# A gated long-convolution and MLP kernel: a filter fold in three operations, a product unit split by output block, and a new instruction order

## The chip, the cores and the metric

The kernel runs on one core of a Trainium2 chip. A core has five engines with an instruction queue of its own each: TensorE (PE, matrix products into the banks of PSUM), VectorE (DVE, elementwise work), ScalarE (ACT, activations and copies with a scale), GpSimd (POOL) and SyncE (SP). Here POOL computes reciprocal square roots and issues accumulating transfers, and SP issues most other transfers. Engines run beside each other and wait for one another through semaphores.

The metric is the device time of one execution in microseconds. Before the change the median of three runs is 221.62 us (221.31 to 222.36). A smaller time is better.

## The reference

The input is a block `x = A_q` of 2048 tokens by 640 features in bf16. The output mixes two branches by a gate per token: branch A, a long convolution over tokens by FFT, and branch B, a layer norm, a GELU product, shifts by one or two tokens, a second product, and an MLP.

```python
def _A_ref(q, k, v, shift_k, ssm_k, ssm_D):
    ...                                    # k_shift: 4 taps over tokens, per feature
    kv = k_shift * v
    kv_pad = jnp.pad(kv, ((0, 0), (0, S), (0, 0)))
    kf_pad = jnp.pad(ssm_k, ((0, 0), (0, S)))
    ...                                    # kv_f, kf_f: real FFTs of length 2 S over the tokens
    y_f = kv_f * kf_f[None, :, :, :]
    y = ...                                # inverse FFT, the first S tokens, in bf16
    y = y + kv * ssm_D[None, None, :]
    return q * y

def _B_ref(x, w1, w2, w3, w4):
    h = _gelu(_layernorm(x, axis=-1) @ w1)
    ...                                    # four quarters of h, shifted by +1, -1, +2, -2 tokens
    hs = jnp.concatenate([g0, g1, g2, g3], axis=-1) @ w2
    x1 = x + hs
    h2 = _gelu(_layernorm(x1, axis=-1) @ w3) @ w4
    return x1 + h2

g = _sigmoid((x * gate_w).sum(-1, keepdims=True))
return g * a + (1 - g) * b
```

The term `kv * ssm_D` is a convolution too, whose filter has D at its first place and zeros elsewhere; so D can be added to the first element of the filter `ssm_k`.

## The kernel before

**Branch A.** The 640 features are five chunks of 128, one feature per partition; `c` is a chunk from 0 to 4. Per chunk, `chunk(c)` (line 1102) issues these steps in turn. `h_load` loads the filter of 2048 taps as four blocks of 512. `h_fold` (line 763) folds each block onto itself, sums and differences of mirrored halves, so that a transform of half the size does. A DMA transpose turns the fold; `h_even` and `h_chunk` finish the filter's transform with products by constant tables (`Re_h`, `Ro_h`, made in `_folded_dft`) and ACT copies the results into `HF`. `k_load`, `v_load`, `kv`, `kv2`, `x_fwd` and `combine` do the same for `k_shift * v`, into `XF`. `unit(c)` (line 1017) then multiplies the two transforms of a chunk: there are four blocks of each, a block of the output is the sum over pairs of an input and a filter block, and each complex product is formed from three real ones (arrays `ACC` and `TT`, with three parts). It works through two halves, output blocks 2 and 3 first and then 0 and 1; in a half, `a` runs over the filter blocks. Some of the sums `ACC += TT` are not DVE instructions but accumulating transfers on POOL. At the end of a half, two operations write the real and imaginary part of the two output blocks into `XF` and a third sets one partition's row. `final(g, o, q, k)` (line 1043) does the inverse transform of output block `o` for group `g` of chunks (chunks 0 to 2, then 3 and 4) by PE, with ACT, DVE and a second PE product (`flip`) behind it, multiplies by q and the gate, and adds it to the output.

**Branch B.** `ln1`, `mm1`, `mm2`, `ln2`, `mm3` and `mm4` do the norms and products of B over 16 tiles of 128 tokens. In `mm1` (line 929) four feature blocks of 128 go into `hT`; the 32 features left over of each quarter come together as a fifth product, and four copies of 32 partitions put them into `hT` at the shift of their quarter (line 946 on DVE, line 944 as a transfer on SP). `mm2` adds onto `X` (line 980, DVE). `base(t)` scales a tile's first 384 columns and stores them to the output through SP; `mm4(t)` overwrites that tile of `X` on ACT and accumulates it onto the output through POOL.

**The order.** The functions only record operations. `schedule` (line 271) then issues them in the order of a list, `SEQUENCE` (line 486), which holds the number of every operation; each engine's queue follows that list. `PLACES` (line 546) says which PSUM bank each product gets, and `ON` (line 553) switches single operations between two engines, in the order in which `turn` (line 677) was called: a scaled copy between ACT and DVE, a sum between DVE and a transfer, a copy of `mm1` between DVE and SP. `emit` (line 301) finds which earlier operations each one depends on and puts in the waits.

The helpers `tt` (line 660), `ts` (line 665) and `act` (line 670) record most operations, so one line of the profile holds many; PE's products are line 692.

Of the kernel before, what the change touches and what calls it, by code (L numbers as in the profile page):

```python
# [407 lines left out]
def _folded_dft():  # L408
# [22 lines left out]
            np.where(first, np.sin(np.pi * kodd / 2), -np.sin(w * 2 * kodd * p))]  # L431
    alt, one = (-1.) ** p, p == 0
    even[0][:, 0:1], even[1][:, 0:1] = (alt - 1) / 2, 0
    even[2][:, 0:1], even[3][:, 0:1] = one, (alt + 1) / 2
    odd = [np.cos(w * bo * p), -np.cos(w * bo * n1), -np.sin(w * bo * n0), -np.sin(w * bo * n1)]
    Rh = np.concatenate(even + odd, 1)
# [10 lines left out]
def bass_gated_mix__ssm_conv_h3__mixer_s_mlp__prompt_kernel(  # L447
# [34 lines left out]
    def ps(n, cls):  # L482
# [3 lines left out]
    SEQUENCE = [1, 4, 5, 6, 26, 7, 3, 45, 24, 8, 0, 49, 50, 51, 55, 48, 68, 9, 10, 11, 12, 13, 14, 15, 16, 69, 17,  # L486
# [66 lines left out]
    ON = ("0000000011111111011011111111111100010000010000101111000000000000001000010010000100000100000100000000"  # L553
          "0000000000000000000000000000000")

    HW = S + 4
    oXF = alloc(20480)
# [611 lines left out]
```

## Time and profile before

| | |
|---|---|
| median of three runs | 221.62 us (221.31 to 222.36) |
| profiled execution | 222.27 us |
| its span, first to last instruction | 220.2 us |
| DVE busy, instructions | 212.1 us (96%), 418 |
| PE busy, matmuls | 209.0 us (95%), 1401 seen |
| ACT busy, instructions | 196.5 us (89%), 326 |
| POOL busy, instructions | 45.7 us (21%), 48 |

The profile is one execution. An engine is busy while an instruction of it runs; a wait is put down to what ended it. In a row of the timeline the first number is the start in the span and the second the duration; several instructions of one shape that follow each other are merged, with their count after x. In a row of groups, the two numbers behind the count are the busy time in us and the mean duration in ns, and then the idle time just before them. A few matmul records are missing from the trace.

### The profile page before, as it was taken

What the parts mean: (1) busy time and instruction counts of PE and PEld (TensorE: products, weight loads), DVE (VectorE), ACT (ScalarE), POOL (GpSimd) and SP (SyncE); (2) the same over time, 40 slices, a digit from 0 to 9 for tenths busy, and PEclk for the clock granted to TensorE, in tenths of its full rate; (3) what the DMA queues carried; (4) which work ended last, traced back from release to release, by engine and by line L of the source; (5) the groups of instructions that cost most, each with busy time, mean ns of one, the idle gap of its engine ahead of it and who ended that gap; (6) DMA issues with size and microseconds to landing.
All of it is one profiled execution on the core that took longest, in us unless ns stands there. A gap on an engine that the chain in (4) does not pass through costs nothing.

```text
span 220.2 us, 3837 instructions
## 1 busy us (share of the span) xinstructions
PE 209.0 (95%) x1401; PEld 125.7 (57%) x1410; DVE 212.1 (96%) x418; ACT 196.5 (89%) x326; POOL 45.7 (21%) x48
## 2 busy tenths in 40 slices
PE   6899999999999999999999999999999999999961
PEld 2598755554664446665446565456665445776730
DVE  5999999999999999999999999999999998999993
ACT  2499999999999999999999999999798978558981
POOL 1331102400010001001380103331101060645440
PEclk9999999999999999999999999999999999999995
DMA  6999998999979995898486893793198299366696
GB/s 170 346 233 214 246 207 231 177 236 193 284 246 204 383 198 95 162 174 185 120 147 110 201 193 43 163 174 71 19 160 182 65 219 246 39 74 71 74 179 119
DMA packets 79440, 37.73 MB, mean 171 GB/s; under 512 B 59001, under 2 KB 76990, under 8 KB 79422
## 3 DMA queue, kind: packets, MB, share of 16 engines
q1 hardware_dynamic: 73920, 31.91, 63.3%
q0 software_dynamic: 5328, 5.51, 18.9%
q8 instruction: 11, 0.18, 0.3%
q10 hardware_dynamic: 174, 0.07, 0.2%
q14 instruction: 7, 0.06, 0.1%
HBM read 14.88 MB, written 5.77 MB: 94 GB/s over the span
## 4 chain that ended last, share of the span: by engine, by line
DVE 57%; PE 28%; DMA 5%; ACT 5%; issue 3%; SPq 0%
DVE arena L660 46%; PE PSall L692 28%; ACT arena L670 5%; DVE arena L665 4%; DMA arena<-arena 3%; DVE arena L861 3%; DVE arena L980 2%; DMA arena<-in_A_q_dram 2%; DVE arena L946 1%; DVE arena L862 0%; DVE arena L866 0%; SPq L237 0%; DVE arena L735 0%; DVE arena L704 0%
## 5 line engine op out<-in xcount | busy, mean ns | idle before, releaser
L692 PE MATMUL PSall<-arena 128*128 128x512 bf16 (+5 forms) x1340 | 201.7, 309 | 3.4 <-ACT arena L670 1.3
L660 DVE TENSOR_TENSOR arena<-arena 128x1024 bf16<-128x1024 bf16 (+14 forms) x270 | 175.1, 712 | 1.7 <-DMA arena<-arena 0.9
L692 PEld LDWEIGHTS PSall<-arena 128*128 128x128 bf16 x1349 | 121.6, 98 | 82.7 <-ACT arena L670 3.3
L670 ACT ACTIVATE arena<-PSall 128x512 bf16<-128x512 f32 (+7 forms) x157 | 94.1, 659 | 9.6 <-PE PSall L750 4.9
L670 ACT ACTIVATE arena<-arena 128x640 bf16<-128x640 bf16 (+5 forms) x107 | 93.5, 904 | 1.9 <-DVE arena L660 1.8
L237 POOL DMA_DIRECT2D out_dram<-arena x24 | 24.1, 1133 | 67.7 <-ACT arena L670 51.7
L869 POOL TENSOR_TENSOR arena<-arena 128x2 f32<-128x2 f32 (+2 forms) x15 | 17.3, 1157 | 58.0 <-DVE arena L866 42.3
L670 ACT ACTIVATE arena<-PSall,arena 128x640 bf16<-128x640 f32 (+2 forms) x32 | 20.5, 652 | 6.8 <-PE PSall L692 6.6
L237 POOL DMA_DIRECT2D arena<-arena x5 | 4.9, 978 | 43.2 <-DVE arena L660 43.2
L980 DVE SCALAR_TENSOR_TENSOR arena<-PSall,arena 128x640 bf16<-128x640 f32 x16 | 12.9, 816 | 0.3
L665 DVE TENSOR_SCALAR arena<-arena 128x640 bf16<-128x640 bf16 (+6 forms) x35 | 11.9, 358 | 0.1
L861 DVE BATCH_NORM_STATS2 arena<-arena 128x6 f32<-128x320 bf16 x20 | 9.0, 484 | 1.3 <-DMA arena<-in_A_q_dram 1.3
L715 PE MATMUL PSall<-arena 128*128 128x512 bf16 x15 | 5.4, 529 | 2.2 <-DVE arena L712 2.2
L670 ACT ACTIVATION_READ_ACCUMULATOR arena<-arena 128x1 f32 x28 | 5.7, 204 | 0.0
L946 DVE TENSOR_SCALAR arena<-arena 32x256 bf16<-32x256 bf16 (+1 forms) x22 | 5.3, 240 | 0.4
L715 PEld LDWEIGHTS PSall<-arena 128*128 128x128 bf16 x15 | 1.8, 128 | 5.0 <-issue 2.5
L922 PE MATMUL PSall<-arena 128*128 128x128 bf16 x40 | 3.4, 220 | 0.9 <-DVE arena L665 0.9
L922 PEld LDWEIGHTS PSall<-arena 128*128 128x128 bf16 x40 | 2.4, 97 | 1.3 <-DVE arena L665 1.3
L866 DVE SCALAR_TENSOR_TENSOR arena<-arena 128x2 f32<-128x2 f32 (+2 forms) x19 | 2.9, 155 | 0.0
L718 ACT ACT_TABLE_LOAD x1 | 1.3, 1283 | 1.3 <-PEq L1154 1.3
L862 DVE BATCH_NORM_AGGREGATE arena<-arena 128x2 f32<-128x12 f32 x10 | 1.7, 192 | 0.0
L980 DVE DVE_READ_ACCUMULATOR arena<-PSall,arena 128x1 f32 x16 | 1.3, 80 | 0.0
(19 smaller groups left out, 2.9 us busy)
## 6 DMA issues: line engine op xcount, KB each, us to landing
arena<-in_A_ssm_k_dram SPq DMA_DIRECT2D x5, 512.0 KB, 5.2
arena<-in_A_q_dram SPq DMA_DIRECT2D x6, 320.0 KB, 5.7
arena<-in_B_w_dram SPq DMA_DIRECT2D x1, 1920.0 KB, 8.4
out_dram<-arena SPq DMA_DIRECT2D x16, 96.0 KB, 3.9
arena<-arena POOLq DMA_DIRECT2D x4, 384.0 KB, 5.0
out_dram<-arena POOLq DMA_DIRECT2D x16, 96.0 KB, 3.6
arena<-in_A_q_dram SPq DMA_DIRECT2D x8, 192.0 KB, 4.1
out_dram<-arena POOLq DMA_DIRECT2D x8, 192.0 KB, 4.0
```

Source lines behind the costliest of these rows:

```text
L237: fn = lambda e: e.dma_start(out, in_, **kw)
L660: P.op(eng, lambda e: e.tensor_tensor(o, real(a), real(b), op), [a, b], [o], dve_ns(o, [a, b], 2) if eng == "dve" else 500)
L665: P.op(eng, lambda e: e.tensor_scalar(o, real(a), s1, s2, op0=op0, **({} if op1 is None else {"op1": op1})), [a] + aps, [o], dve_ns(o, [a] ...
L670: P.op("act", lambda e: e.activation(real(o), real(a), f, bias=bias, scale=scale, **({"accum_out": accum} if accum is not None else {})), ...
L692: fns.append(lambda e, l=l, r=r, i=i: e.matmul(real(o), l, r, start=(i == 0), stop=(i == last)))
L715: P.op("pe", lambda e: e.matmul(real(pw), warm[:, 0:128], warm[:, 128:640], start=True, stop=True), [warm], [pw], 427.0 if i < 14 else 216.0)
L861: P.op("dve", lambda e, o=o, i=i: e.bn_stats(o, i), [i], [o], 400)
L866: P.op("dve", lambda e: e.scalar_tensor_tensor(o, a, x, b, op0=op0, op1=op1), [a, b] + aps, [o], n_of(o) / 0.96 + 65)
L869: P.op("pool", lambda g: g.tensor_tensor(o, a, e, ALU.pow), [a, e], [o], dur)
L922: P.op("pe", [lambda e, c=c, pb=pb, xn=xn: e.transpose(real(pb)[:, 128 * c:128 * (c + 1)], xn[:, 128 * c:128 * (c + 1)], ident) for c in r ...
L946: P.op("dve", lambda e, o=hT[q, 4, c0:c0 + n], i=hx[q, :]: e.tensor_scalar(o, i, 1.0, None, op0=ALU.mult), [hx[q, :]], [hT[q, 4, c0:c0 + n ...
L980: P.op("dve", lambda e: e.scalar_tensor_tensor(x, real(pr), 1.0, x, op0=ALU.mult, op1=ALU.add, accum_out=st[1, 0][:, t:t + 1]), [pr, x], [ ...
```

## The change

There are four parts.

1. **The fold.** The D term is no longer added to the filter's first element by an operation of its own. A small constant array `skip` holds zero and D, and the third operation, which used to copy the two unpaired elements of each block, adds `skip` to them. The two large operations now run over 128 elements where they ran over 127, and so also produce the element that two small operations made; its sign in the difference is the other one, and the constant tables turn it back. The last run writes one element beyond the fold, so each chunk of `HF` gets 16 elements of padding (`HS`).
2. **The last half of unit 4.** For chunk 4 output blocks 1 and 0 are worked out one after the other instead of together.
3. **The copies of `mm1`** on DVE now name the neighbouring column of `hT` as read, so that they wait for the block before.
4. **Order, banks and switches.** `SEQUENCE` and `PLACES` are new lists, and `ON` differs in three places: of the tokens 768 to 1023 the last copy moves from SP to DVE, of the tokens 1024 to 1535 the second moves from SP to DVE and the third from DVE to SP.

```diff
+    even[5][0] *= -1
...
+    odd[1][0] *= -1
...
-    HW = S + 4
+    HW, HS = S + 4, 4096 + 16
...
-    oHF = alloc(20480)
+    oHF = alloc(5 * HS)
...
-    dgT = bfs[:, 32:42]
-    Dcol, gwT = dgT[:, 0:5], dgT[:, 5:10]
+    skip = bfs[:, 0:40].rearrange("p (c e b) -> p c e b", c=5, e=2)
+    gwT = bfs[:, 48:53]
...
+    P.op("dve", lambda e: e.memset(skip, 0.0), [], [skip], 70)
...
-    act(dgT, pr, ACTF.Copy)
+    act(skip[:, :, 1, 0], pr[:, 0:5], ACTF.Copy)
+    act(gwT, pr[:, 5:10], ACTF.Copy)
...
     def h_fold(c):
         k, fo = kst[c], kfo[c]
-        tt(k[:, 0, 0:1], k[:, 0, 0:1], Dcol[:, c:c + 1], ALU.add)
         kh = k.rearrange("p b (h i) -> p b h i", h=2)
-        fh = fo.rearrange("p e b (h i) -> p e b h i", h=2)
         for e, op in ((0, ALU.add), (1, ALU.subtract)):
-            tt(fh[:, e, :, :, 1:128], kh[:, :, :, 1:128], kh[:, :, ::-1, 255:128:-1], op)
-            tt(fo[:, e, :, 128], k[:, :, 384], k[:, :, 128], op)
-        ts(fo[:, :, :, 0], kh.rearrange("p b h i -> p h b i")[:, ::-1, :, 0], 1.0, None, ALU.mult)
+            f = fo[:, e, :, 1:129]
+            tt(bass.AP(f.tensor, f.offset, [f.ap[0], [256, 4], [128, 2], [1, 128]]), kh[:, :, :, 1:129], kh[:, :, ::-1, 255:127:-1], op)
+        tt(fo[:, :, :, 0], kh.rearrange("p b h i -> p h b i")[:, ::-1, :, 0], skip[:, c], ALU.add)
         P.dma(sp, het[c].rearrange("p e b k c -> p (e b k) c"), fo.rearrange("p e b n -> p (e b n)"), transpose=True)
...
-                         [hx[q, :]], [hT[q, 4, c0:c0 + n]], n / 3.84 + 65)
+                         [hx[q, :], hT[q, 4, c0 - 1:c0]], [hT[q, 4, c0:c0 + n]], n / 3.84 + 65)
...
-    ADDS = ()
+    ADDS, LAST = (), 4
     def unit(c):
...
-        for o0 in (2, 0):
-            for a in range(o0 + 2):
+        for o0, o1 in ((2, 4), (0, 2)) if c < LAST else ((2, 4), (1, 2), (0, 1)):
+            for a in range(o1):
                 lo = max(o0, a)
-                n, x0 = o0 + 2 - lo, lo - a
-                acc, tmp = ACC[:, lo - o0:2], TT[:, 0:n]
+                n, x0 = o1 - lo, lo - a
+                acc, tmp = ACC[:, lo - o0:o1 - o0], TT[:, 0:n]
...
-            Y = XF[:, c, o0:o0 + 2]
-            tt(Y[:, :, 0], ACC[:, :, 2], ACC[:, :, 1], ALU.subtract)
-            tt(Y[:, :, 1], ACC[:, :, 2], ACC[:, :, 0], ALU.add)
-            scale(Y[0:1, :, :, 0:128], ACC[0:1, :, 0:2, 0:128], 1.0, True)
+            Y, R = XF[:, c, o0:o1], ACC[:, 0:o1 - o0]
+            tt(Y[:, :, 0], R[:, :, 2], R[:, :, 1], ALU.subtract)
+            tt(Y[:, :, 1], R[:, :, 2], R[:, :, 0], ALU.add)
+            scale(Y[0:1, :, :, 0:128], R[0:1, :, 0:2, 0:128], 1.0, True)
```

The lists are as long as the program (1171 numbers before, 1163 after) and are left out. By the new list, with each operation set against its old number: the product adds of `mm2` for tiles 5 to 9, `combine(3)`'s second half, and on ACT several `base` copies come earlier on their queues; on POOL the accumulates of `mm4` for tiles 0, 1 and 3 come much later (places 38, 35 and 30 of 44 instead of 13, 17 and 14), and on SP the store of `base(10)` stands after four loads of q and a transpose.

More of the change, by code (lines that the diff above doesn't have):

```diff
@@ L572, in bass_gated_mix__ssm_conv_h3__mixer_s_mlp__prompt_kernel @@
     XF = V(oXF, 20480).rearrange("p (c b r n) -> p c b r n", c=5, b=4, r=2)
-    HF = V(oHF, 20480).rearrange("p (c b r n) -> p c b r n", c=5, b=4, r=2)
+    HF = [V(oHF + HS * c, 4096).rearrange("p (b r n) -> p b r n", b=4, r=2) for c in range(5)]
     hT = V(oHT, DC * HW).rearrange("p (c s) -> p c s", c=DC)
@@ L598, in bass_gated_mix__ssm_conv_h3__mixer_s_mlp__prompt_kernel @@
     four = lambda o: V(o, 2048).rearrange("p (e b k c) -> p e b k c", e=2, b=4, k=2)
-    kst = [V(oHF + 4096 * c, 2048).rearrange("p (b n) -> p b n", b=4) for c in range(5)]
-    kfo = [V(oHF + 4096 * c + 2048, 2048).rearrange("p (e b n) -> p e b n", e=2, b=4) for c in range(5)]
+    kst = [V(oHF + HS * c, 2048).rearrange("p (b n) -> p b n", b=4) for c in range(5)]
+    kfo = [V(oHF + HS * c + 2048, 2048).rearrange("p (e b n) -> p e b n", e=2, b=4) for c in range(5)]
     KT = [V(oXF + 4096 * c, 2048) for c in range(5)]
     VT = [V(oXF + 4096 * c + 2048, 2048) for c in range(5)]
-    TD = [V(oHF + 4096 * c + 2048, 2048) for c in range(5)]
-    TA, TB = V(oB + 8192, 2048), [V(oHF + 4096 * c, 2048) for c in range(5)]
+    TD = [V(oHF + HS * c + 2048, 2048) for c in range(5)]
+    TA, TB = V(oB + 8192, 2048), [V(oHF + HS * c, 2048) for c in range(5)]
     sdT = [four(oXF + 16384 if c < 4 else oHF) for c in range(5)]
     het = [four(oXF + 18432 if c < 4 else oHF + 2048) for c in range(5)]
-    evn = [V(oHF + 16384 if c < 4 else oHF + 4096, 2048).rearrange("p (o e b c) -> p o e b c", o=2, e=2, b=4) for c in range(5)]
-    eft = [V(oHF + 18432 if c < 4 else oHF + 6144, 2048).rearrange("p (m e b c) -> p m e b c", m=2, e=2, b=4) for c in range(5)]
+    evn = [V(oHF + 4 * HS if c < 4 else oHF + HS, 2048).rearrange("p (o e b c) -> p o e b c", o=2, e=2, b=4) for c in range(5)]
+    eft = [V(oHF + 4 * HS + 2048 if c < 4 else oHF + HS + 2048, 2048).rearrange("p (m e b c) -> p m e b c", m=2, e=2, b=4) for c in range(5)]
     ACC, TT = [V(oB + 3072 * i, 3072).rearrange("p (o m n) -> p o m n", o=2, m=3) for i in range(2)]
@@ L613, in bass_gated_mix__ssm_conv_h3__mixer_s_mlp__prompt_kernel @@
     pair = lambda o, n: V(o, 2 * n).rearrange("p (t d) -> p t d", t=2)
-    qA = [pair(oHF + 8192 + 768 * k if k < 5 else oHF + 4096 + 768 * (k - 5), 384) for k in range(8)]
-    qB = [pair(oHF + 12288 + 512 * k, 256) for k in range(8)]
+    qA = [pair(oHF + 2 * HS + 768 * k if k < 5 else oHF + HS + 768 * (k - 5), 384) for k in range(8)]
+    qB = [pair(oHF + 3 * HS + 512 * k, 256) for k in range(8)]
     abA = [pair(oW2 + 768 * i, 384) for i in range(4)]
@@ L618, in bass_gated_mix__ssm_conv_h3__mixer_s_mlp__prompt_kernel @@
     abB = [pair(oB + 8192 + 512 * i, 256) for i in range(8)]
-    gyB = [pair(oHF + 16384 + 512 * i, 256) for i in range(8)]
+    gyB = [pair(oHF + 4 * HS + 512 * i, 256) for i in range(8)]
     sm = V32(oSm, 388)
```

12 lines of the change are left out of this document (6 added, 6 removed), and 129 rows, old and new, of tables (PLACES, SEQUENCE).

## The prediction

> **What bounds the kernel now.** I read the page's first two parts, then the waits of VectorE (DVE), then busy times by stage.
>
> ```profile
> span 220.2 us, 3837 instructions
> PE 209.0 (95%) x1401; PEld 125.7 (57%) x1410; DVE 212.1 (96%) x418; ACT 196.5 (89%) x326; POOL 45.7 (21%) x48
> DVE  5999999999999999999999999999999998999993
> ...
> 10.00:211.00 201.00, 199.69 (x1348) 121.38 (x1355) 198.70 (x368) 189.63 (x313) 41.79 (x39) 1.00 0.83 169
> 211.00:221.00 10.00, 2.30 (x13) 0.89 (x10) 5.84 (x21) 3.67 (x8) 1.19 (x1) 0.66 0.68 132
> ...
> DVE arena L861 <- DMA arena<-in_A_q_dram: 1.3, 2, 0.9
> DVE arena L660 <- DMA arena<-arena: 0.9, 1, 0.9
> DVE arena L660 <- ACT arena L670: 0.2, 1, 0.2
> ```
>
> In the two rows that begin with a stretch of time the columns are PE, PEld, DVE, ACT, POOL (busy us and instructions), granted clock, DMA share, GB/s. Between 10 and 211 us DVE works 198.70 of 201.00 us and TensorE (PE) 199.69: both are full, and ACT is nearly so. In the last 10 us PE has 13 matmuls left and DVE still 5.84 us of work. The waits of DVE that have a name come to 2.4 us (1.3, 0.9, 0.2). So DVE carries the end, with PE right beside it. The time can fall by what DVE no longer issues, as far as PE keeps pace, and it rises by any new wait on DVE. Since everything hangs on DVE instructions, their price comes first.
>
> ```profile
> 93.84 0.68 DVE L660 TENSOR_TENSOR arena<-arena 128x1024 bf16<-128x1024 bf16 x1
> 94.45 0.18 DVE L665 TENSOR_SCALAR arena<-arena 128x8 bf16<-128x8 bf16 x1
> 94.52 1.02 DVE L660 TENSOR_TENSOR arena<-arena 128x4 bf16<-128x4 bf16 x2
> ...
> 14.67 0.69 DVE L660 TENSOR_TENSOR arena<-arena 128x1016 bf16<-128x1016 bf16 x1
> 15.28 0.48 DVE L861 BATCH_NORM_STATS2 arena<-arena 128x6 f32<-128x320 bf16 x1
> ...
> 18.01 0.18 DVE L660 TENSOR_TENSOR arena<-arena 128x4 bf16<-128x4 bf16 x1
> 18.09 0.49 DVE L861 BATCH_NORM_STATS2 arena<-arena 128x6 f32<-128x320 bf16 x1
> ...
> 27.69 0.22 DVE L946 TENSOR_SCALAR arena<-arena 32x256 bf16<-32x256 bf16 x1
> 27.94 0.69 DVE L660 TENSOR_TENSOR arena<-arena 128x1024 bf16<-128x1024 bf16 x1
> ```
>
> Columns: start, duration. An instruction overlaps the next by some 0.08 us: one of 8 elements lasts 0.18 but the next starts 0.07 later (94.45, 94.52); one of 4 elements holds the queue 0.08 (18.01, 18.09); the 1016-element fold lasts 0.69 and holds it 0.61; a 32x256 copy 0.25. Steps, not durations, add up on a full engine.
>
> **The change part by part.** *The fold.* Per chunk it issued one add of D (128x1), two large folds, two 128x4 operations, one 128x8 copy, and now two large folds and one 128x8 add. Three instructions fewer in each of five chunks: 15 x 0.07 = 1.05 us less. The bounds are 0.6 (the first two chunks are folded before 40 us, where a later wait could swallow their share) and 2.4 (by durations, as if nothing overlapped: the rows below give 150 + 2 x 166 + 181 - 181 = 482 ns per chunk). I take 1.05, since these instructions stand in a full queue. The large folds grow from 1016 to 1024 elements: 682 against 680 ns, so 0.02 us for ten.
>
> ```profile
> L660 DVE TENSOR_TENSOR arena<-arena 128x1024 bf16<-128x1024 bf16 x80 | 52.0, 682 | 1.0 <-DMA arena<-arena 0.9
> L660 DVE TENSOR_TENSOR arena<-arena 128x2048 bf16<-128x2048 bf16 x40 | 48.1, 1214 | 0.1
> L660 DVE TENSOR_TENSOR arena<-arena 128x1536 bf16<-128x1536 bf16 x16 | 15.1, 947 | 0.2 <-ACT arena L670 0.2
> L660 DVE TENSOR_TENSOR arena<-arena 128x512 bf16<-128x512 bf16 x22 | 9.0, 417 | 0.1
> L660 DVE TENSOR_TENSOR arena<-arena 128x1016 bf16<-128x1016 bf16 x10 | 6.7, 680 | 0.0
> L660 DVE TENSOR_TENSOR arena<-arena 128x4 bf16<-128x4 bf16 x10 | 1.6, 166 | 0.0
> L665 DVE TENSOR_SCALAR arena<-arena 128x8 bf16<-128x8 bf16 x5 | 0.9, 181 | 0.0
> L660 DVE TENSOR_TENSOR arena<-arena 128x1 bf16<-128x1 bf16 x5 | 0.8, 150 | 0.0
> ...
> ACT arena L670 <- PE PSall L750: 4.9, 1, 4.9
> ```
>
> *Constants.* One more small memset falls before the first tokens have landed (the 1.3 us of DVE's wait for them covers it; without that cover it is one step, 0.07). One ACT copy becomes two; ACT waits 4.9 us there for PE's line 750, so it costs nothing, and 0.1 us of ACT if that cover is gone. The padded rows of HF and the changed signs in the constant tables issue nothing.
>
> *Copies of mm1.* Three switches flip: the last copy of tokens 768 to 1023 goes from an SP transfer to DVE (+0.25), and of tokens 1024 to 1535 one 512-wide copy goes to DVE and another to SP (0). The new read of the neighbouring column makes each copy wait for the same partitions' copy of the block before; in the new order other instructions stand between each such pair, and the one that waits for a transfer (tokens 1536 on, third group) is issued more than ten DVE instructions after it. 0 us; from above 0.25 per pair, should one become adjacent.
>
> *The last half of unit 4.* Before, DVE did one 2048, four 1024, one 512 and one 1536: 1214 + 4 x 682 + 417 + 947 = 5306 ns. After, three of 1024, three of 512, one 1536 and four more of 512: 3 x 682 + 7 x 417 + 947 = 5912. Of the 0.61 us, four more overlaps of 0.08 go off: +0.29 us. ACT's row copy becomes two half ones, beside PE and DVE work. Between 0.29 and -0.4 (output block 1 is ready before block 0, so the inverse matmuls of the last group need not wait for all): I take 0.29, since DVE, not PE, still has the work at 211 us.
>
> *The order.* Operations that wait for the very one before them pay extra: in the first two rows below the aggregation reads what the statistics before it wrote and starts 0.51 us after it; in the last two the aggregation is that of another tile and starts 0.41 after it.
>
> ```profile
> 3.48 0.48 DVE L861 BATCH_NORM_STATS2 arena<-arena 128x6 f32<-128x320 bf16 x1
> 3.99 0.21 DVE L862 BATCH_NORM_AGGREGATE arena<-arena 128x2 f32<-128x12 f32 x1
> ...
> 5.52 0.50 DVE L861 BATCH_NORM_STATS2 arena<-arena 128x6 f32<-128x320 bf16 x1 [0.34 <-DMA arena<-in_A_q_dram]
> 5.93 0.19 DVE L862 BATCH_NORM_AGGREGATE arena<-arena 128x2 f32<-128x12 f32 x1
> ```
>
> So 0.1 us each. Going through both sequences I find 11 such neighbours on DVE before and 7 after: -0.4 us. The 0.9 us wait for a transfer between buffers is the accumulate of unit 3; the new order puts some 0.2 us more DVE work behind its issue: -0.2. On the other side, DVE's residual adds of mm2 tiles 6, 8 and 9 move up: 135 DVE instructions (readouts of the accumulator included) stand ahead of tile 9's, and 413 matmuls run up to the end of that tile.
>
> ```profile
> 0.00:47.60 47.60, 44.10 (x412) 29.52 (x414) 44.65 (x136) 40.14 (x92) 10.29 (x15) 1.00 0.98 230
> 0.00:48.90 48.90, 45.40 (x418) 30.04 (x420) 45.95 (x138) 41.44 (x93) 10.29 (x15) 1.00 0.99 230
> ```
>
> Today DVE has issued 136 and PE 412 at the same 47.60 us, so the matmuls come just as the add wants them: between 0 and 1.3 us of wait (if the matmuls ahead are the wide ones and PE needs until 48.90). I take +0.3, nearer the count.
>
> On POOL the accumulates of mm4 tiles 0, 1 and 3 move from about 103 us to near the end, behind ACT results long done, each holding POOL 1.1 us.
>
> ```profile
> L237 POOL DMA_DIRECT2D out_dram<-arena x24 | 24.1, 1133 | 67.7 <-ACT arena L670 51.7
> ```
>
> POOL sits idle 67.7 us before these 24 and is busy for 45.7 of 220 in all, so 3.4 us more of it late is hidden: 0. Were that cover gone, only the group-0 accumulates queued behind them would come later, and they are not the last to land.
>
> **Sum**, on the profiled execution (222.27 us; span 220.2 and 2.1 around it): -1.05 + 0.02 + 0.25 + 0.29 - 0.4 - 0.2 + 0.3 = -0.8. The profiled run is 0.65 above the median of 221.62 (221.31 to 222.36), so by medians 221.62 - 0.8 = **220.8 us**.
>
> **Rivals.** *Nothing gained (221.6):* PE's matmuls are the same in number and size, it has only 1.3 us to spare of 201, and if it paces the middle, DVE's saved steps turn into waits for it. Against it: in the last 10 us DVE has 5.84 us of work and PE 2.30.
>
> *Slower (223.1):* the store of base 10 now stands on SP's queue behind four loads of q and a transpose. ACT's mm4 of tile 10 overwrites the rows which that store reads, and waits for its landing. Between the two, ACT has mm4 of tile 9, the row copy of h_even, base 15 and one 1024-wide copy.
>
> ```profile
> DMA to landing us min/median/max: 1.6/3.7/7.8
> ...
> 156.08 0.78 ACT L670 ACTIVATE arena<-PSall,arena 128x640 bf16<-128x640 f32 x1
> 157.98 1.73 ACT L670 ACTIVATE arena<-PSall 128x768 bf16<-128x768 f32 x2 [1.12 <-PE PSall L692]
> 163.24 1.00 ACT L670 ACTIVATE arena<-PSall 128x1024 bf16<-128x1024 f32 x1
> 164.14 0.60 ACT L670 ACTIVATE arena<-arena 128x384 bf16<-128x384 bf16 x1
> 167.75 0.79 ACT L670 ACTIVATE arena<-PSall,arena 128x640 bf16<-128x640 f32 x1 [0.91 <-PE PSall L692]
> ```
>
> That work is 0.8 + 1.0 + 0.6 + 1.0 = some 3.4 less overlaps, 3.0 us; stores land 3.7 us after issue in the middle, 7.8 at most. ACT idles 1.12 and 0.91 us near there, which takes up 2.0. So it decides from a landing of 5 us on, and at 7.8 costs 2.8, of which some 2.3 would reach DVE through the chunk-4 copies behind it: 220.8 + 2.3.
>
> *More than that (219.7):* of the 2.3 us that DVE is not busy between 10 and 211 the order saves another half (1.1).
>
> *The fold falls out of the fast rate (226):* the starts at element 1 could cost it. From 1024 to 2048 elements a product grows by 1214 - 682 = 532 ns; at half that rate a 1024-element fold takes 0.53 more, ten 5.3 us. The 1016-element fold starts at element 1 too and takes 680 ns, as the even ones do, so I give it little. The Trainium skill, VectorE: DVE Perf Modes, section on Mode 2x_1P, asks for 16-bit data, step of one and 4-byte alignment for two results per cycle, and by that sentence the new fold would be slow; the old one, misaligned in the same way, is not, so the trace does not agree.
>
> **How the numbers follow.** About 0.5% (1.1 us) is what a measurement here can tell from no change: faster means below 220.5, slower above 222.7. The forecast has 0.45 with its own range of 219.9 to 221.7 (0.20 of it faster, 0.25 same); nothing gained 0.13 (0.11 same, 0.02 slower); base 10's store 0.17 (0.16 slower, 0.01 same); more than that 0.20, faster; the slow fold 0.03 and what I have not seen 0.02, slower. Faster 0.40, same 0.37, slower 0.23. Cases of both signs hold the chance, so the range reaches from 219.2 (the larger gain and half a microsecond of its spread) to 223.0 (the store).
>
> **What would show it.** Right: 409 DVE instructions instead of 418 (15 fewer in the folds, 4 more in unit 4, one copy, one memset), busy near 211.5 us, fold rows of 128x1024 at 682 ns, no wait of DVE over 1 us beside the accumulate of unit 3 and the first tokens, and the last DVE instruction about 0.8 us earlier. Wrong: waits of DVE for PE around 47 us of more than 1.3, an idle ACT before mm4 of tile 10, folds of 1.2 us, or a last stage in which PE and ACT, not DVE, are late.

## The result, and the profile after

The changed kernel takes 221.75 us in the median of 20 runs (220.60 to 222.49), the kernel before 221.76 (221.10 to 222.40). The ratio is 0.9991 with a 95% interval of 0.9975 to 1.0006, that is 0.2 us less, between 0.55 less and 0.13 more. The forecast had 0.8 less. In these runs single executions of one kernel lie up to about 1 us on either side of its median. Two executions of the experiments took over 1.5% more than the fastest of their kernel and are in no ratio, though their clock was no lower than that of others: one of four of all_less (223.04 us) and one of twelve of pow_tap (224.54 us). The profiled execution of the changed kernel (220.93 us) is 0.8 below its median, that of the kernel before (222.27) 0.5 above, so the two spans say nothing about the change. What follows compares waits, and takes the profiles of several kernels together where they share an order.

From the page of the changed kernel: the span, the busy times with their numbers of instructions, and by stretch of time the busy us (and instructions) of PE, PEld, DVE, ACT and POOL, the granted clock, the DMA share and GB/s. Then DVE's waits: us in total, how many, the longest. Last, groups of DVE instructions of one shape: how many, busy us, mean ns, idle time before them. The helpers stand one line lower than before: L661, L671 and L981 are what L660, L670 and L980 were (in split_alone and order_alone, L658 and L668 are the first two).

```profile
span 219.1 us, 3837 instructions
PE 208.5 (95%) x1402; PEld 125.9 (57%) x1410; DVE 211.1 (96%) x409; ACT 196.7 (90%) x328; POOL 51.2 (23%) x48
```

```profile
10.00:211.00 201.00, 199.22 (x1340) 121.32 (x1345) 198.83 (x361) 190.16 (x312) 47.36 (x39) 1.00 0.84 169
211.00:221.00 10.00, 1.65 (x9) 0.80 (x9) 5.13 (x19) 2.82 (x7) 1.40 (x2) 0.65 0.68 125
```

```profile
DVE arena L862 <- DMA arena<-in_A_q_dram: 1.6, 2, 1.0
DVE arena L867 <- POOL arena L870: 0.9, 1, 0.9
...
DVE arena L661 <- DMA arena<-in_A_ssm_k_dram: 0.4, 1, 0.4
```

```profile
L661 DVE TENSOR_TENSOR arena<-arena 128x1024 bf16<-128x1024 bf16 x89 | 58.1, 680 | 0.5 <-DMA arena<-in_A_ssm_k_dram 0.4
...
L661 DVE TENSOR_TENSOR arena<-arena 128x512 bf16<-128x512 bf16 x28 | 11.4, 416 | 0.0
...
L661 DVE TENSOR_TENSOR arena<-arena 128x8 bf16<-128x8 bf16 x5 | 0.9, 180 | 0.0
```

DVE issues 409 instructions instead of 418, the folds run at 680 ns, and DVE is 1.0 us less busy (211.1 against 212.1). Unit 3's wait of 0.9 us for a transfer between buffers is gone. In its place stand a wait of 0.9 us for POOL, which the kernel before did not have, and one of 0.4 us for a filter load.

These sums can be made exact. The next table adds up, for each profile, the step from each DVE instruction's start to the next; the usual step of a shape (the lower quartile over all profiles) is work, what goes beyond is waiting, put down by the time (us from the start) at which it ended; the stretch from 66 to 78 us has none anywhere and is left out. It is worked out from the traces, in us.

```
                  work  first   -12  12-43  43-52  52-57  57-66  78-82  83-120 120-170 170-190  190-
                        start
before          208.50   3.07  0.71   1.00   0.14   0.13   0.55   0.11    0.58    0.27    0.99  0.80
fold_alone      207.44   3.06  0.27   1.26   0.04   0.13   0.77   0.11    0.81    0.54    0.77  0.82
split_alone     208.77   3.12  1.00   1.02   0.14   0.12   0.41   0.10    0.58    0.27    0.43  2.24
changed kernel  207.73   3.40  0.83   1.16   0.11   0.66   0.04   1.02    0.22    0.35    0.01  0.60
order_alone     208.44   3.40  0.12   1.26   0.54   0.60   0.03   1.03    0.22    0.35    0.01  2.20
order_split     208.84   3.37  0.42   1.15   0.72   0.30   0.03   1.02    0.23    0.35    0.01  0.61
pow_moved       207.66   3.25  0.24   1.26   0.94   0.73   0.04   0.01    1.11    0.43    0.01  0.61
old front, 6           3.06  0.64   1.16   0.11   0.15   0.69
new front, 12          3.37  0.63   1.25   0.64   0.68   0.06
```

The last two rows are means over the kernels (below) that have the order of before, or of the changed kernel, in the first 66 us, without all_less and pow_load. The work came out as forecast for the fold, -1.06 (before to fold_alone), and for the split, +0.27 (before to split_alone). For the order it is -0.06 (before to order_alone) or +0.07 (split_alone to order_split), that is nothing. The new order takes away waits at 57 to 66 us (-0.6), at 83 to 120 (-0.4), at unit 3 (170 to 190 us: 0.43 to 0.99 in the four profiles with the old order throughout, of which fold_and_split has 0.56; 0.7 in the mean) and at the tail (-0.2). It brings waits for transposes and a filter load at 43 to 57 us (+1.1 in the mean; the changed kernel's own profile happens to show only half of it), for POOL at 80 us (+0.9), and DVE's first statistics start 0.3 later. So DVE saves about 0.8 of work and loses some 0.4 in waits, which leaves a gain within the measured interval (0.55 less to 0.13 more).

### The profile page after: what moved, and what is told of

It reads as the page before. It is cut to its first block, busy times and chain, and to the rows that moved or that the text cites. A ratio compares the mean times of both kernels' runs of the same rounds, so it can differ in the third digit from the quotient of the medians.

```text
span 219.1 us, 3837 instructions
## 1 busy us (share of the span) xinstructions
PE 208.5 (95%) x1402; PEld 125.9 (57%) x1410; DVE 211.1 (96%) x409; ACT 196.7 (90%) x328; POOL 51.2 (23%) x48
## 4 chain that ended last, share of the span: by engine, by line
DVE 77%; PE 8%; DMA 5%; POOL 3%; SPq 2%; issue 2%; ACT 1%; DVEq 0%
DVE arena L661 68%; PE PSall L693 8%; POOL arena L870 3%; DVE arena L981 3%; DMA arena<-in_A_q_dram 3%; DVE arena L862 2%; DVE arena L666 2%; DMA arena<-in_A_ssm_k_dram 2%; DVE arena L947 1%; SPq L234 1%; SPq L237 1%; ACT arena L671 1%; DVE arena L867 1%; DVE arena L863 0%; DVE arena L737 0%
## 5 line engine op out<-in xcount | busy, mean ns | idle before, releaser
L661 DVE TENSOR_TENSOR arena<-arena 128x1024 bf16<-128x1024 bf16 (+11 forms) x264 | 174.3, 723 | 0.7 <-DMA arena<-in_A_ssm_k_dram 0.4
L671 ACT ACTIVATE arena<-PSall 128x512 bf16<-128x512 f32 (+7 forms) x158 | 93.4, 651 | 5.7 <-PE PSall L693 2.2
L671 ACT ACTIVATE arena<-arena 128x640 bf16<-128x640 bf16 (+6 forms) x108 | 93.2, 896 | 2.7 <-DVE arena L661 1.7
L870 POOL TENSOR_TENSOR arena<-arena 128x2 f32<-128x2 f32 (+2 forms) x15 | 22.2, 1483 | 79.7 <-DVE arena L867 63.1
L237 POOL DMA_DIRECT2D out_dram<-arena x24 | 24.6, 1253 | 30.6 <-ACT arena L671 20.0
L671 ACT ACTIVATE arena<-PSall,arena 128x640 bf16<-128x640 f32 (+2 forms) x32 | 20.3, 653 | 7.5 <-PE PSall L693 7.4
L981 DVE SCALAR_TENSOR_TENSOR arena<-PSall,arena 128x640 bf16<-128x640 f32 x16 | 12.8, 811 | 0.0
L666 DVE TENSOR_SCALAR arena<-arena 128x640 bf16<-128x640 bf16 (+5 forms) x30 | 11.1, 386 | 0.1
L671 ACT ACTIVATION_READ_ACCUMULATOR arena<-arena 128x1 f32 x28 | 5.6, 198 | 0.0
L981 DVE DVE_READ_ACCUMULATOR arena<-PSall,arena 128x1 f32 x16 | 1.2, 76 | 0.0
```

The lines of the kernel that those rows point to most:

```text
L237: fn = lambda e: e.dma_start(out, in_, **kw)
L661: P.op(eng, lambda e: e.tensor_tensor(o, real(a), real(b), op), [a, b], [o], dve_ns(o, [a, b], 2) if eng == "dve" else 500)
L666: P.op(eng, lambda e: e.tensor_scalar(o, real(a), s1, s2, op0=op0, **({} if op1 is None else {"op1": op1})), [a] + aps, [o], dve_ns(o, [a] ...
L671: P.op("act", lambda e: e.activation(real(o), real(a), f, bias=bias, scale=scale, **({"accum_out": accum} if accum is not None else {})), ...
L870: P.op("pool", lambda g: g.tensor_tensor(o, a, e, ALU.pow), [a, e], [o], dur)
L981: P.op("dve", lambda e: e.scalar_tensor_tensor(x, real(pr), 1.0, x, op0=ALU.mult, op1=ALU.add, accum_out=st[1, 0][:, t:t + 1]), [pr, x], [ ...
```

## The experiments

Each difference is taken against the kernel before, run beside it on the same chip; ratios have their 95% interval. A difference between two kernels of the table is the difference of their ratios, times 221.8 us.

**The three parts, one by one.** In the first two kernels the order, banks and switches stay those of before; the numbers of removed operations drop out of the list, new ones stand where the old ones stood.

```diff
 fold_alone: kernel before, with
-        tt(k[:, 0, 0:1], k[:, 0, 0:1], Dcol[:, c:c + 1], ALU.add)
...
+            tt(bass.AP(f.tensor, f.offset, [f.ap[0], [256, 4], [128, 2], [1, 128]]), kh[:, :, :, 1:129], kh[:, :, ::-1, 255:127:-1], op)
+        tt(fo[:, :, :, 0], kh.rearrange("p b h i -> p h b i")[:, ::-1, :, 0], skip[:, c], ALU.add)
```

> Only the new fold, in the order, on the banks and with the switches of before. Theory A (the terms of the prediction add up, the new order gives the gain back): 1.0 us under before (15 small VectorE instructions by 0.07 go). Rival B (PE is full, so saved VectorE time does not come off the end): within 0.3 us of before. Rival C (the terms are right but smaller: a small VectorE instruction costs less than 0.07 in its place): 0.3 to 0.6 under before.

```diff
 split_alone: kernel before, with
-        for o0 in (2, 0):
+        for o0, o1 in ((2, 4), (0, 2)) if c < LAST else ((2, 4), (1, 2), (0, 1)):
```

> Only unit 4's last half split by output block, in the order of before, the block that is done later directly behind the first. Theory A: 0.3 us over before (five instructions more by 0.06). Rival B: within 0.3 of before, or under it if the first block's transforms start earlier and it is PE that waits for them. Rival C: 0.1 to 0.3 over before.

```diff
 fold_and_split: kernel before, with both edits above
```

> The new fold and the split unit in the order, on the banks and with the switches of before. Theory A: 0.7 us under before, that is 0.5 under the changed kernel, which has the new order besides. Rival B: within 0.3 of before. Rival C: 0 to 0.4 under before.

```diff
 order_alone: changed kernel, with the old fold and
-        for o0, o1 in ((2, 4), (0, 2)) if c < LAST else ((2, 4), (1, 2), (0, 1)):
+        for o0 in (2, 0):
...
```

> The order, the banks and the three switches of the changed kernel with the old fold (its parts directly behind each other where the new ones stand) and the old unit. Theory A: 0.5 us over before (the waits that the new order makes: 0.9 for POOL's power, 0.4 for a filter load, 0.6 for a first load, less the 0.9 at unit 3 that is gone, and what the prediction gave to the order). Rival B: within 0.3 of before. Rival C: 0 to 0.4 over before.

```diff
 order_split: changed kernel, with the old fold
-            tt(bass.AP(f.tensor, f.offset, [f.ap[0], [256, 4], [128, 2], [1, 128]]), kh[:, :, :, 1:129], kh[:, :, ::-1, 255:127:-1], op)
+            tt(fh[:, e, :, :, 1:128], kh[:, :, :, 1:128], kh[:, :, ::-1, 255:128:-1], op)
+            tt(fo[:, e, :, 128], k[:, :, 384], k[:, :, 128], op)
...
```

> The changed kernel with the old fold, its seven parts where the new four stand. Theory A: 1.0 us over the changed kernel (15 small instructions by 0.07). Rival B: within 0.3 of it. If the new order is worth something with the old fold too: not over before.

```
                       order of before             order of the changed kernel
neither                1                           1.0076 (1.0046 to 1.0105)  order_alone
new fold               0.9981 (0.9962 to 1.0001)   not run
split                  1.0062 (1.0028 to 1.0096)   1.0031 (1.0013 to 1.0049)  order_split
both                   1.0065 (1.0037 to 1.0092)   0.9991 (0.9975 to 1.0006)  the change
```

None of the theories gets all of this: order_split came as theory A said (0.9 us over the changed kernel), fold_alone is nearest to rival C, and what the split and the order cost without each other, and fold and split together, no theory foretold. The fold is worth 0.4 us in the old order (-0.0019, up to 0.8) and 0.9 in the new (-0.0040); the forecast's 1.05 lies beyond the first and within the spread of the second. The split costs 1.4 us in the old order and saves 1.0 in the new, though by the table its work on DVE is 0.27 and 0.40. And the new order without the other two parts is 1.7 us slower. Split and order pay only together, and the stage from 199 us on shows why. First PE in split_alone, then in order_alone, then in the changed kernel: start, duration, number of matmuls, idle time and what ended it.

```profile
198.83 6.31 PE L690 MATMUL PSall<-arena 128*128 128x256 bf16 x48
206.08 1.48 PE L690 MATMUL PSall<-arena 128*128 128x384 bf16 x10 [0.94 <-DVE arena L658]
```

```profile
198.82 4.25 PE L690 MATMUL PSall<-arena 128*128 128x256 bf16 x33
203.72 3.75 PE L690 MATMUL PSall<-arena 128*128 128x256 bf16 x25 [0.66 <-DVE arena L658]
207.68 5.26 PE L690 MATMUL PSall<-arena 128*128 128x384 bf16 x41 [0.21 <-DVE arena L658]
```

```profile
198.81 12.08 PE L693 MATMUL PSall<-arena 128*128 128x256 bf16 x93
```

In the changed kernel PE runs 93 matmuls without a stop. There, by the lists and the traces, DVE's four instructions of block 0 lie between 202.79 and 205.28 us, with instructions of the last stage between them. In split_alone the four stand in one row, from 203.94 to 205.75 us, and the subtraction over 384 elements that PE's next product waits for starts behind them, at 205.67: PE stands for 0.94 us, and DVE waits 2.24 us behind 190 (table above) instead of 0.60. With one undivided half in the new order (order_alone) PE stands for 0.66 and 0.21, and DVE waits 2.20. Block 0 spread out in the old order was not tried.

**POOL's power.** The wait for POOL in the changed kernel, seen from both sides: the power in the kernel before and DVE beside it, then the power in the changed kernel and DVE beside that.

```profile
63.30 1.01 POOL L869 TENSOR_TENSOR arena<-arena 128x4 f32<-128x4 f32 x1 [21.56 <-DVE arena L866]
...
63.47 0.82 DVE L980 SCALAR_TENSOR_TENSOR arena<-PSall,arena 128x640 bf16<-128x640 f32 x1
```

```profile
72.96 7.14 POOL L870 TENSOR_TENSOR arena<-arena 128x4 f32<-128x4 f32 x1 [31.34 <-DVE arena L867]
```

```profile
72.74 0.14 DVE L867 SCALAR_TENSOR_TENSOR arena<-arena 128x4 f32<-128x4 f32 x1
72.81 6.42 DVE L661 TENSOR_TENSOR arena<-arena 128x1024 bf16<-128x1024 bf16 x7
80.13 0.16 DVE L867 SCALAR_TENSOR_TENSOR arena<-arena 128x4 f32<-128x4 f32 x1 [0.91 <-POOL arena L870]
```

The same power over 128x4 numbers takes 1.01 us beside a residual add that reads PSUM, and 7.14 beside seven instructions with two operands in SBUF. It ends 0.9 us after the last of them (79.2), once DVE stands still and waits for it. The Trainium skill, SBUF — State Buffer, section "Who interferes with whom", says that a VectorE instruction with two SBUF inputs contends with a GpSimd instruction that reads SBUF, and that one with at most one SBUF input, outside the two-port modes, does not; the trace agrees (7.14 against 1.01). The test moves the instruction that starts the power in front of such a residual add:

```diff
 pow_moved: changed kernel
-    SEQUENCE = [... 437, 622, 586, 594, 587, 574 ... 804, 805, 380, 531, 532, 591 ...]
+    SEQUENCE = [... 437, 622, 586, 531, 532, 594, 587, 574 ... 804, 805, 380, 591 ...]
```

> The changed kernel with one VectorE instruction (the one that makes the variances of token tiles 4 to 7) moved four places up, in front of the residual add of mm2's tile 12, and POOL's power behind it. POOL's power took 7.14 us at 73 us and ended only when VectorE stood still, with seven two-input VectorE instructions between SBUF and SBUF over it; the residual add reads PSUM, and beside such an add the power took 1.01 us before. Theory A (VectorE sets the end and the 0.98 us that it waited for POOL is what the new order costs): power under 1.5 us, no wait, 0.7 to 1.0 us under the changed kernel, 0.9 to 1.2 under before. Rival B (PE sets the end): the wait goes, the time stays within 0.3 of the changed kernel. Rival D (POOL's power is long whatever stands beside it): power still some 7 us, ends at 76, wait gone as well, time as under A.

```profile
69.52 1.01 POOL L870 TENSOR_TENSOR arena<-arena 128x4 f32<-128x4 f32 x1 [28.62 <-DVE arena L867]
...
108.92 1.83 DVE L661 TENSOR_TENSOR arena<-arena 128x2047 bf16<-128x2047 bf16 x2 [0.79 <-ACT arena L671]
```

The power is down to 1.01 us and DVE's wait for it is gone. That the power is long whatever stands beside it has fallen. But 0.79 us of waiting stand at 108.9 us now, for ACT (by the table 1.0 less at 78 to 82 us, 0.9 more at 83 to 120). The time is 0.9965 (0.9938 to 0.9992): 0.8 us under before, and 0.6 under the changed kernel with intervals that overlap; it lies between what theory A (0.7 to 1.0 under the changed kernel) and rival B (within 0.3) foretold, and decides for neither. It is the only complete kernel here whose interval lies below 1. Two kernels build on it.

```diff
 pow_tap: pow_moved, chunk 3's fourth tap on VectorE instead of ACT
-    ON = (... switch 47: "0" ...)
+    ON = (... switch 47: "1" ...)
```

> The kernel in which POOL's power is moved up, and besides chunk 3's fourth tap on VectorE (0.75 us) instead of ACT (1.99 us). With the power moved up VectorE waited 0.88 us for this tap at 108.9 us, where the 0.98 us of the power's wait had been given back. Theory E: this wait goes, and 0.0 to 0.6 us comes off against the kernel with the power moved up alone, that is 0.8 to 1.4 under before. If VectorE alone set the time: 0.75 more than with the power alone less 0.88 of wait, so no change. If PE is what is left at 109 us: within 0.2 of the power alone, with new waits for PE right behind.

The wait at 108.9 us went, and the time did not fall: 1.0001 (0.9974 to 1.0028), 0.8 us over pow_moved (-0.05 to 1.65 by the two intervals; its runs lie between 220.5 and 223.5 us). Theory E, which had 0.8 to 1.4 under before, is a miss. "No change" against pow_moved lies at the edge of the interval, so between the other two this one decides nothing.

```diff
 pow_load: pow_moved, chunk 2's filter load (386) earlier on SP's queue
-    SEQUENCE = [... 277, 352, 279, 386, 261 ...]
+    SEQUENCE = [... 386, 248 ... 277, 352, 279, 261 ...]
```

> The changed kernel with POOL's power moved up, and the load of chunk 2's filter issued three transposes earlier on SP's queue (at 41 us, as before, in place of 49). Theory H: the waits at 54 and 80 us both go, 0.2 to 0.5 us under the kernel with the power alone. Theory E: the wait for ACT at 108.9 grows by as much, time within 0.2 of the power alone.

A miss for both theories: 1.0026 (1.0008 to 1.0043), 1.4 us over pow_moved. SP's queue in pow_moved, then SP and DVE in pow_load:

```profile
41.52 5.38 SPq L234 DMA_TRANSPOSE arena<-arena  x3
```

```profile
41.84 0.58 SPq L237 DMA_DIRECT2D arena<-in_A_ssm_k_dram  x1
42.46 5.95 SPq L234 DMA_TRANSPOSE arena<-arena  x3
...
51.26 0.69 DVE L661 TENSOR_TENSOR arena<-arena 128x1024 bf16<-128x1024 bf16 x1 [1.83 <-DMA arena<-arena]
```

The load no longer makes DVE wait at 54 us. But it stands in front of the three transposes that follow (in the kernel before, one of the transposes here was ahead of it); SP is done with them 1.5 us later (48.41 against 46.90), and DVE waits 1.83 us for the last of them. So this one move exchanges a wait for a longer one. Whether another place for the load avoids both was not tried.

**Which engine sets the time.** What comes off an engine was left out of the changed kernel, or done twice, on one engine and on several.

```diff
 dve_less, dve_act_less, all_less, pe_dve_less
-        tt(SX, X4[:, :, 0], X4[:, :, 1], ALU.add)
+        w = 512 if c == 0 else 64
+        tt(SX[:, :, 0:w], X4[:, :, 0, 0:w], X4[:, :, 1, 0:w], ALU.add)
 pe_less, all_less, pe_dve_less
-                    pairs = [(Ro[:, r, kk, 128 * m:128 * (m + 1)], t[:, 1 - r, :, kk]) for kk in range(2)]
+                    pairs = [(Ro[:, r, kk, 128 * m:128 * (m + 1)], t[:, 1 - r, :, kk]) for kk in range(2 if c == 0 else 1)]
 act_less, dve_act_less, all_less
-            scale(o, k, taps[:, j, c:c + 1], TAPS[j])
+            w = 1024 if j == 3 and c else 2048
+            scale(o[:, 0:w], k[:, 0:w], taps[:, j, c:c + 1], TAPS[j])
 dve_more
+        if c:
+            tt(SX, X4[:, :, 0], X4[:, :, 1], ALU.add)
 pe_more: in mm(), for the odd columns of chunks 1 to 4
+        [lambda e: e.matmul(real(o), *pairs[0], start=True, stop=True)] + fns
```

> The changed kernel with VectorE work left out: the sum of two spectra in units 1 to 4 is made over 64 of 512 columns, the rest is what the unit before left. Four instructions of 2048 elements become 256: 0.95 us each, 3.8 in all, between 93 and 183 us; PE and ACT keep their work. Theory A (VectorE sets the end): 3 to 3.8 under the changed kernel. Rival B (PE sets the end): under 0.5. In between: both engines are near the bound, and the share that comes off says how near.

> The changed kernel with PE work left out: the second of two products is left out in the forward transforms of the odd columns of chunks 1 to 4, 16 matmuls of 128x512 by 0.22 to 0.31 us, 3.5 to 5 us of PE; VectorE and ACT keep their work. Theory A: within 0.5 us of the changed kernel. Rival B: 3 us or more under it.

> The changed kernel with ACT work left out: the fourth tap of chunks 1 to 4 is scaled over 1024 of 2048 columns, 0.95 us less each, 3.8 in all; the other half is what the second tap left. VectorE and PE keep their work. Theory E (VectorE, PE and ACT are all full from 40 to 160 us, and what one of them saves comes back as waits for the other two): within 0.5 us of the changed kernel, as with less work on VectorE alone (0.3 under) and on PE alone (0.0). Rival G (ACT is the one that sets the time): 2 us or more under it.

> The changed kernel with the work left out on VectorE (3.8 us in four instructions) and on ACT (3.8 us in four) together. Theory E: PE is then the last of the three, so 0.3 to 1.5 us under the changed kernel. If VectorE's waits for ACT were the only thing that ate its saving: 2 to 3.5 under. Rival F (a transfer sets the time): within 0.3.

> The changed kernel with the work left out on PE (16 matmuls of 216 ns, 3.5 us) and on VectorE (four instructions shortened, 3.8 us), ACT keeping its own. If PE and VectorE are the two full engines: as with all three, 1.5 to 2.5 us under the changed kernel. If ACT is as full as they are: within 0.5 of it.

> The changed kernel with the work left out on VectorE, on ACT and on PE (16 matmuls) together. Theory E: 2.5 to 3.8 us under the changed kernel, though each alone gave 0.0 to 0.3. Rival F (a transfer or a queue sets the time): within 0.5 of it.

> The changed kernel with the sum of two spectra made twice in units 1 to 4 (four more VectorE instructions of 2048 elements by 1.13 us, 4.5 us). Theory E (VectorE is full too): 3.5 to 4.5 us over the changed kernel. If PE alone sets the time: under 2 us over it.

> The changed kernel with 16 matmuls done twice (128x512, chunks 1 to 4, odd columns of the forward transforms; 216 ns from one start to the next, 3.5 us). Theory E (PE is full): 2.5 to 3.5 us over the changed kernel. If PE has slack behind VectorE: under 1 us over it.

```
                 work changed, us              ratio to before              us against the changed kernel
dve_less         DVE -3.7                      0.9985 (0.9959 to 1.0011)    -0.1
pe_less          PE -3.5                       0.9999 (0.9973 to 1.0025)    +0.2
act_less         ACT -3.4                      0.9991 (0.9974 to 1.0007)     0.0
dve_act_less     DVE -3.7, ACT -3.4            0.9998 (0.9978 to 1.0018)    +0.2
pe_dve_less      PE -3.5, DVE -3.7             0.9980 (0.9951 to 1.0009)    -0.2
all_less         PE -3.5, DVE -3.7, ACT -3.4   0.9904 (0.9874 to 0.9935)    -1.9
dve_more         DVE +4.5                      1.0198 (1.0164 to 1.0232)    +4.6
pe_more          PE +3.5                       1.0199 (1.0147 to 1.0252)    +4.6
```

The work changed is what the traces show, DVE by the table's way of counting; ACT's four shorter instructions took 1.16 us instead of 2.00 each, so 3.4 us less and not the 3.8 expected. Taken away from one engine, or from two, the work gives nothing that can be measured (PE and ACT together was not run). Taken from all three it gives 1.9 us; that row rests on three executions (219.60, 220.39 and 220.72 us). Added to DVE or PE, it costs in full; adding to ACT was not tried. Theory A (DVE sets the end), the single rivals (PE does, ACT does) and rival F (a transfer does) have all fallen: three engines are full side by side. The sizes that theory E gave for less work were too large, though: it had 0.3 to 1.5 us for DVE and ACT together and 2.5 to 3.8 for all three. The stretch from 100 to 160 us shows it, first of the kernel before, then of the changed one, then of dve_less (columns as above: PE, PEld, DVE, ACT, POOL), and dve_less's wait of DVE for ACT.

```profile
100.00:160.00 60.00, 59.89 (x344) 33.60 (x345) 59.72 (x87) 58.59 (x82) 15.62 (x14) 1.00 0.67 129
```

```profile
100.00:160.00 60.00, 59.79 (x346) 33.93 (x348) 59.93 (x83) 59.59 (x83) 12.62 (x10) 1.00 0.68 143
```

```profile
100.00:160.00 60.00, 60.00 (x344) 33.38 (x342) 56.95 (x81) 59.52 (x82) 12.61 (x10) 1.00 0.69 143
```

```profile
DVE arena L661 <- ACT arena L671: 4.0, 6, 0.9
```

In dve_less DVE is busy 3.0 us less in these 60 us, and PE and ACT are as full as they were: the 3.7 us came back as 4.0 us of waiting for ACT. With ACT's work left out as well, PE remains. Of the 3.4 us that is the least saving of the three, 1.9 arrive; where the rest stays was not traced. In pe_more (the last row below) DVE waits just as long for ACT, though neither of the two has more to do than in the changed kernel: PE, ACT and DVE feed each other there, and one late engine delays the others.

```profile
DVE arena L661 <- ACT arena L671: 4.0, 5, 1.0
```

**The old front with the new tail.** Both kernels have the new fold and the split, and the order of before up to a joint.

```diff
 front_old (front_old_longer): changed kernel
-    SEQUENCE = [new order]
+    SEQUENCE = [order of before, without the last 408 (293) operations of the new order] + [those 408 (293), in the new order]
```

> New fold and split unit; up to 141 us the order, banks and switches of before, from there those of the changed kernel. Theory H (the new order pays in the front, for POOL's power 0.98 and for a transpose and a filter load at 50 to 54 us some 0.6, and gains behind 180 us, where unit 3's wait of 0.97 goes): both gains and no loss, 0.7 of fold less split and 0.7 of unit 3's wait, 1.0 to 1.5 us under before. Theory E (PE, ACT and VectorE are all full to 160 us, so that what VectorE no longer waits for in the front comes back as another wait): 0 to 0.4 under before, as the changed kernel. If the new order loses nothing in the front: not under the changed kernel.

> The same with the joint at 166 us in place of 141. Theory H: within 0.3 us of the kernel with the joint at 141, since no wait of the one order lies between. If what counts is the order between 141 and 166 us (products of mm4 and their stores): they differ by over 0.5.

They are slower, 1.0055 (1.0036 to 1.0074) and 1.0085 (1.0059 to 1.0110). Neither theory said so, and they do not decide between them, because the joint itself costs: of front_old the stretch from 120 to 140 us, and DVE's waits for ACT.

```profile
120.00:140.00 20.00, 18.14 (x110) 10.43 (x109) 19.93 (x28) 19.79 (x29) 2.97 (x3) 1.00 0.66 132
```

```profile
DVE arena L660 <- ACT arena L670: 1.7, 5, 0.7
```

PE loses 1.9 us of 20 just ahead of the joint, in one wait for ACT that ends at 139.2 us (fold_and_split, with the old order throughout, has PE busy for 20.00 us there). Presumably what PE would have done there ahead of time stands behind the joint in the new tail; that was not tested. In front_old_longer the loss lies behind its joint: DVE waits 2.0 us between 170 and 190 us. Whether the old front would be better with a tail that fits it stays open.

## Why the prediction was wrong

**Outcome.** Foretold were 220.8 us, 0.8 under before. Measured was no difference that can be told (0.2). The rival "nothing gained (221.6)" is the one that came, in its time; its mechanism (PE paces the middle) came only in part, as said below. None of the signs that the prediction named for being wrong came.

**What was right.** The number of DVE instructions (409) came as foretold, and the busy time nearly so (211.1 against some 211.5). The fold's term was -1.05 and its work on DVE -1.06. The split's term was +0.29 and its work +0.27. The larger folds run at 680 ns, so the rival of the slow fold (226) is out. The -0.4 for neighbours was of the right size. The table's work can't show it, since what a neighbour adds to a usual step counts there as waiting; but DVE steps that are 50 to 150 ns above the usual of their shape come to 2.9 us in 27 steps before and to 2.45 in 23 in order_alone, worked out from the traces. The +0.25 for mm1's copy is one more 32x256 copy (16 instead of 15), and small. One reading was short: DVE's named waits of 2.4 us leave out 0.8 us at the very start, on which nothing hangs.

**The step that failed: the order.** It was costed with neighbours (-0.4), unit 3's wait (-0.2) and mm2's adds (+0.3), so -0.3 in all. By the table its waits in the changed kernel come to some +0.4: 1.9 us of waits go and 2.3 come.

- Unit 3's wait went altogether: 0.99 to 0.01 by the table. The step was mis-sized by 0.8 in the cautious direction.
- The adds of mm2's tiles 8 and 9 start at 47.49 and 48.84 us without waiting for PE. The +0.3 was not there. DVE of the changed kernel:

```profile
47.49 0.82 DVE L981 SCALAR_TENSOR_TENSOR arena<-PSall,arena 128x640 bf16<-128x640 f32 x1
...
48.84 0.82 DVE L981 SCALAR_TENSOR_TENSOR arena<-PSall,arena 128x640 bf16<-128x640 f32 x1
```

- The waits that the new order makes were not in the sum at all: POOL's power (+0.9), transposes at 43 to 52 us and the filter load of chunk 2 at 54 (+1.1 in the mean of 12 profiles against 6), a first start 0.3 later. The prediction followed POOL only for its transfers near the end and SP only for base 10's store. The power of ln2 for tiles 4 to 7 was moved in front of a row of two-operand DVE instructions, and the load of chunk 2's filter behind three transposes on SP; both moves stand in the lists, and neither was priced.
- The sum adds the parts as if they were independent, and they are not: the order alone costs 1.7 us, and on top of fold and split it gains 1.6 (1.0065 to 0.9991); the split, +0.29 in the sum, costs 1.4 in the one order and gains 1.0 in the other.

**The premise that failed.** "The time can fall by what DVE no longer issues, as far as PE keeps pace" left ACT out. The prediction quoted 189.63 of 201 us for ACT and called it nearly full; from 100 to 160 us it was at 58.59 of 60 already. The rival "nothing gained" named PE as the one that paces the middle. The runs show that it is not PE alone: 3.5 us less of PE gave nothing, 3.7 less of DVE gave nothing, and DVE and ACT both with 3.4 to 3.7 less gave nothing.

**The other rivals.** Base 10's store did no harm. ACT of the changed kernel has no gap in front of mm4's tile 10, the second row:

```profile
157.49 1.00 ACT L671 ACTIVATE arena<-PSall 128x1024 bf16<-128x1024 f32 x1
158.39 0.77 ACT L671 ACTIVATE arena<-PSall,arena 128x640 bf16<-128x640 f32 x1
```

"More than that" (219.7) did not come. The split's term left open a gain of up to 0.4 because the last group of inverse matmuls starts earlier; in the new order that gain is larger (1.0 us against the undivided half in the same order), and in the old order it turns into a loss of 1.4.

**What is settled and what is not.** Settled: the work terms; that POOL's power is long because of what stands beside it; that DVE, PE and ACT are full together, so that less work on one of them, or on DVE and one other, is not seen. Not settled: how much of the 0.9 us at POOL comes off the end when it is removed (0.6 by the ratios, with an interval that reaches from 1.3 less to 0.1 more); whether a front without the new waits would keep its gain; and why the fold's 1.06 us of DVE, spread over five chunks up to 139 us, comes off the end in the new order (0.9, between 0.4 and 1.4) when 3.7 us taken out in four places between 93 and 183 us does not.

## What to carry to other kernels

Look at the busy shares by stretch, not over the whole span: where three engines are at about 98% or more in the same stretch, as here, a saving on one was paid back as a wait for the next, while work added to VectorE or TensorE cost in full, so a forecast there starts at "nothing" and needs a reason to leave it. Terms of parts that share a queue need not add: what the split was worth changed its sign with the order around it. When an order changes, list for every queue (POOL's small operations and SP's loads among them) what now stands beside and in front of each moved instruction, not only what it depends on. With a split that lets a consumer start early, look at what stands behind the second part on the producer's queue: here it paid where instructions that feed the consumer stood between the second part's own, and cost where they stood behind them.

## What the runs showed of the hardware

A POOL instruction over 128x4 numbers can take 7.14 us instead of 1.01 only because VectorE runs two-operand instructions between SBUF buffers beside it, without a gap; it ended 0.9 us after VectorE stood still. In the twelve profiles that have the new front the transposes at 43 to 52 us made VectorE wait between 0.1 and 1.0 us, in six with the old front never more than 0.3, so one profile of a kernel can miss or show such a wait by chance. Sixteen extra matmuls of 216 ns (3.5 us) made the kernel 4.6 us longer (3.4 to 5.8 by the two intervals): no part of it was hidden by the other engines, and whether it cost more than its own time is not settled.
